# Placing the odd linear product and the mirroring pass within a unit of a fused FNet-mixing and maxout-FFN kernel

## The chip, the cores and the metric

The kernel runs on one core of a Trainium2 chip. The metric is the device time of one execution in microseconds, as the median of several executions. TensorE (PE) multiplies, VectorE (DVE) and ScalarE (ACT) work on what it leaves in PSUM, GpSimd (POOL) works on SBUF and issues some DMAs, and SyncE (SP) issues the other DMAs. Each engine takes its instructions in the order in which the program lists them, and waits on semaphores where one needs another's result.

## The reference

```python
def _attn_ref(x):                        # x: (8, 3072, 256)
    X = np.fft.fft(x, axis=1)
    X = np.fft.fft(X, axis=2)
    return X.real.astype(np.float32)

def _moe_ref(x, w1, w2, w3, w_out):      # x: (24576, 256), w1..w3: (256, 768), w_out: (768, 256)
    h = np.maximum(np.maximum(x @ w1, x @ w2), x @ w3)
    return (h @ w_out).astype(np.float32)
```

The result of the first is the input of the second: 8 batch entries of 3072 tokens, each of 256 values.

## The kernel before

**What is multiplied.** The kernel never forms the mixed tokens in full. The Fourier transform over the 3072 positions leaves, for each batch entry, two tables of 128 rows and 1536 columns, an even part `tE` and an odd part `tO`; the transform over the 256 features is folded into the weights. A token's values come from the even part plus the odd one, and those of its mirror image (position 3072 less its own) from the even part less the odd one. So one column gives two output rows, a "plus" and a "minus" one. The maximum over three products is written as x·w1 + max(0, x·(w2−w1), x·(w3−w1)). The x·w1 part goes straight to the output through one folded matrix (`gw`), and is called the linear part here. The maximum goes through the 768 hidden columns (`hp` for plus, `hm` for minus) and then through `wout_bf`.

**Batch, block, unit, slot.** A batch entry has 1536 columns in 3 blocks of 512. A block is worked in 6 units, one for each 128 of the 768 hidden columns (`jc` 0 to 5), so an entry has 18 units; "unit 0" to "unit 17" below are those of one entry, and `jc` is the unit's number within its block. A block's 512 columns are also 4 slots of 128 columns, and each slot yields 128 plus rows and 128 minus rows of the output.

**A unit's first half** makes the hidden values. `unit_plus` (L491, L492) runs four matmuls of 512 columns: an even and an odd one into the PSUM tile `pse2`, then an even and an odd one into `pse3`. `unit_out` (L505, L506) then lets ACT write relu(`pse2`) to `stmp`, and DVE write max(`pse3`, `stmp`) to `hp`. One unit later, `finish(prev)` runs the two difference products of the previous unit (`unit_minus`, L499), which add −2 times the odd part to the same two PSUM tiles, and a second `unit_out` that writes `hm`. The tiles `pse2` and `pse3` have two buffers each, so a unit's `pse3` cannot be started until DVE has written the `hm` of the unit two before it, which happens within the unit just before.

**A unit's second half** makes output of the block before it. The generator `l2_block` lists, slot by slot, 12 matmuls of 256 columns (`l2_hidden`, L516): 6 from `hp` and 6 from `hm`, added in a PSUM tile `po`. `l2_some(n)` takes the next n steps of that list. Between two slots of a pair `l2_even` (L528, L531) makes the even linear part of two later slots: two matmuls of 256 columns and a copy by ACT into an SBUF tile, noted in `lines`. The odd linear part is `l2_odd`: one matmul of 257 columns (L539), which is the first to write the slot's `po`; then DVE's mirroring pass `other` (L542), which reads that `po`; then POOL's addition (L545), which makes the minus half of the slot's linear part from `other`. The slot's 12 hidden matmuls add into the same `po`, so they wait until `other` has been made. At the slot's end DVE adds `po` and the linear part into `ot` (L567), POOL issues an indirect DMA for the minus rows (L569) and SP issues the plain stores. There are two `po` buffers. The odd product of a slot therefore waits until the `ot` of the slot two before it is done.

**Where `l2_odd` stands before the change.** In a unit the order is: plus products, odd product and mirroring pass, `hp`, difference products, `hm`, hidden matmuls. It is called in the units with `jc` 1, 2, 4 (slots 1, 2, 3 of the block before) and `jc` 5 (slot 0 of the block at work). The very first block has no such calls for its slot 0: `l2_block` itself calls `l2_even` and `l2_odd` there, in the midst of the hidden matmuls.

**What else is in a unit.** The dictionary `plan` hangs pieces of the next entries' transform to a unit's end: the `s` and `k` matmuls (L445, L447, L471, L473) with an eviction by ACT, fetches of input by SP, and `turn_chunk`, the conversions by POOL (L148, L151) that bring the rows of the entry after next into order. For entries 2 to 6 the `s` and `k` pieces lie in units 5 to 17, one each; for entry 1 they begin in unit 6; in entry 0 they begin in unit 10 and run into entry 1. Conversions lie in units 6 to 17 of an entry and in units 0 to 3 of the next, one part each; those of entry 2 lie in unit 14 of entry 0 to unit 3 of entry 1, two parts each. Entry 7 has no pieces but a short side job in units 0 to 5.

The count that `l2_some` takes in a block's units is 9, 9, 8, 9, 9, 8, and what is left is taken after the last unit's pieces.

Of the kernel before, what the change touches and what calls it, by code (L numbers as in the profile page):

```python
# [33 lines left out]
def kernel(  # L34
# [11 lines left out]
    B, S, D = x.shape  # L46
# [438 lines left out]
    def unit_plus(te, to, jc, n):  # L485

        js = slice(jc * 128, (jc + 1) * 128)
        pse2 = ps_l1.tile([128, TOKB], FP32, name="pse2", tag="pse2")
        pse3 = ps_l1.tile([128, TOKB], FP32, name="pse3", tag="pse3")
        for (pse, i) in ((pse2, 0), (pse3, 1)):  # L490
            nc.tensor.matmul(pse[:, 0:n], gE[i][:, js], te, start=True, stop=False)  # L491
            nc.tensor.matmul(pse[:, 0:n], gO[i][:, js], to, start=False, stop=True)  # L492
        return pse2, pse3

    def unit_minus(pses, to, jc):

        js = slice(jc * 128, (jc + 1) * 128)
        for i, pse in enumerate(pses):
            nc.tensor.matmul(pse, gD[i][:, js], to, start=False, stop=True,  # L499
                             skip_group_check=True)  # L500

    def unit_out(pses, dst, n):
        stmp = h_pool.tile([128, TOKB], BF16, name="stmp", tag="stmp")
        src3 = pses[1][:, 0:n]
        nc.scalar.activation(out=stmp[:, 0:n], in_=pses[0][:, 0:n], func=AX.Relu)  # L505
        nc.vector.tensor_tensor(out=dst, in0=src3, in1=stmp[:, 0:n], op=ALU.max)  # L506

    def stored(st, mine, others):
        for group in others:
            tc.declare_no_dep(st.ins, group=group, reason="each store has rows of its own")  # L510
        tc.add_to_no_dep_group(mine, st.ins)

    def l2_hidden(po, hcols):
        for jc in range(NJC):
            yield
            nc.tensor.matmul(po, hcols(jc), wout_bf[:, jc * 256:(jc + 1) * 256],  # L516
                             start=False, stop=(jc == NJC - 1), skip_group_check=True)

    lines = {}
    odd = {}  # L520

    def l2_even(b, slot):

        pl = ps_f.tile([128, 512], FP32, name="pl", tag="ps")
        for i in range(2):
            ci = (slot + i) * 128
            yield
            nc.tensor.matmul(pl[:, i * 256:(i + 1) * 256], mixes[b].tE[:, ci:ci + 128],  # L528
                             gw[:, 0:256], start=True, stop=True)
        even = even_pool.tile([128, 1024], FP32, name="even", tag="even")  # L530
        nc.scalar.copy(out=even.rearrange("p (i c) -> p i c", i=2)[:, :, 0:256],  # L531
                       in_=pl.rearrange("p (i c) -> p i c", i=2))
        for i in range(2):
            lines[b, slot + i] = even[:, i * 512:(i + 1) * 512]

    def l2_odd(b, slot):

        po = ps_o.tile([128, 512], FP32, name="po", tag="po")
        nc.tensor.matmul(po[:, 0:257], mixes[b].tO[:, slot * 128:slot * 128 + 128], gw[:, 256:513],  # L539
                         start=True, stop=True)  # L540
        other = other_pool.tile([128, 256], FP32, name="other", tag="other")
        nc.vector.scalar_tensor_tensor(out=other, in0=twice, scalar=po[:, 256:257],  # L542
                                       in1=po[:, 0:256], op0=ALU.mult, op1=ALU.subtract)
        line = lines[b, slot]
        nc.gpsimd.tensor_tensor(out=line[:, 256:512], in0=line[:, 0:256], in1=other, op=ALU.add)  # L545
        odd[b, slot] = po

    def l2_block(b, blk, hp, hm):

        base = b * S  # L550
        for sub in range(4):
            slot = blk * 4 + sub
            r = slot + 1
            sp = slice(sub * 128, sub * 128 + 128)
            if (b, slot) not in odd:
                yield from l2_even(b, slot)
                l2_odd(b, slot)
            if sub % 2:
                after = (b, slot + 1) if slot < 11 else (b + 1, 0)
                if after < (B - 1, 8):  # L560
                    yield from l2_even(*after)
            lin = lines.pop((b, slot))
            po = odd.pop((b, slot))
            ot = out_pool.tile([128, 512], FP32, name="ot", tag="ot")
            yield from l2_hidden(po[:, 0:256], lambda jc: hp[:, jc, sp])
            yield from l2_hidden(po[:, 256:512], lambda jc: hm[:, jc, sp])
            nc.vector.tensor_tensor(out=ot, in0=po, in1=lin, op=ALU.add)  # L567
            lo = 1 if r == 12 else 0
            stored(nc.gpsimd.indirect_dma_start(  # L569
                out, bass.IndirectOffsetOnAxis(  # L570
                    ap=rows_m[0:128 - lo, b * 12 + slot: b * 12 + slot + 1], axis=0),
                ot[lo:128, 256:512], None), "scattered", ("scattered", "direct"))
            nc.gpsimd.memset(mark, 0.0)
            if r <= 11:
                stores = [(0, 128, base + r)]
            else:
                stores = [(0, 64, base), (64, 128, base + 12)]
            for (p0, p1, row) in stores:
                stored(nc.sync.dma_start(out=out[row: row + 24 * (p1 - p0 - 1) + 1: 24, :],
                                         in_=ot[p0:p1, 0:256]), "direct", ("scattered",))  # L580
# [71 lines left out]
    def l2_some(n):  # L652
        while n > 0 and l2_queue:
            try:
                next(l2_queue[0])
                n -= 1
            except StopIteration:
                l2_queue.pop(0)
# [85 lines left out]
    for b in range(B):  # L744
        mm = mixes[b]
        tE, tO = mm.tE, mm.tO
        prev = None

        def finish(prev):
            pses, to, jc, hm = prev  # L750
            unit_minus(pses, to, jc)
            unit_out(pses, hm[:, jc, ::-1] if hm is last_hm else hm[:, jc, :], TOKB)

        last_hm = None
        if b == B - 1:
            flipped = []
            for t, name in ((tE, "tEr"), (tO, "tOr")):
                fl = h_pool.tile([128, TOKB], BF16, name=name, tag=name)
                flipped.append(fl)
        for blk in range(3):  # L760
            cs = slice(blk * TOKB, (blk + 1) * TOKB)
            hp = h_pool.tile([128, NJC, TOKB], BF16, name="hp", tag="hp")
            hm = h_pool.tile([128, NJC, TOKB], BF16, name="hm", tag="hm")
            if b == B - 1 and blk == 2:
                last_hm = hm
                for t, fl in zip((tE, tO), flipped):
                    nc.gpsimd.tensor_copy(fl, t[:, 3 * TOKB - 1: 2 * TOKB - 1: -1])
            for jc in range(NJC):
                pses = unit_plus(tE[:, cs], tO[:, cs], jc, TOKB)
                nb, nblk = (b, blk) if jc == 5 else (b, blk - 1) if blk else (b - 1, 2)  # L770
                slot = nblk * 4 + {1: 1, 2: 2, 4: 3, 5: 0}.get(jc, 12)
                if slot < 12 and (0, 0) < (nb, slot) < (B - 1, 8):
                    l2_odd(nb, slot)
                unit_out(pses, hp[:, jc, :], TOKB)
                if prev is not None:
                    finish(prev)
                prev = (pses, tO[:, cs], jc, hm)
                l2_some(8 if jc % 3 == 2 else 9)
                if b == B - 1 and blk == 0:
                    if jc == 0:  # L780
                        middle = l2_mid()
                    for _ in range(5):
                        next(middle, None)
                for fn in plan.get((b, blk * NJC + jc), ()):
                    fn()
            l2_some(1000)
            if blk == 2:
                finish(prev)
            l2_queue.append(l2_last(hp, hm, tE, tO, flipped) if b == B - 1 and blk == 2 else
                            l2_block(b, blk, hp, hm))  # L790

    l2_some(1000)
# [29 lines left out]
```

## Time and profile before

| | |
|---|---|
| Median of 3 executions | 426.38 us (426.24 to 426.39) |
| The profiled execution, its own time | 426.3 us |
| Its span, from the first to the last instruction | 424.4 us |
| Granted TensorE clock, mean | 0.999 |
| Time from the start of one entry's units to the same place of the next, entries 2 to 6 | 48.0 us |

The profile is of one execution. Its rows give the start of an instruction in us from the start of the span, its length, and the idle time before it with what ended that idle time. Matmuls overlap: a matmul of 512 columns is shown as 0.38 us long, yet the next one starts 0.21 us after it. So a wait on TensorE is read from the distance between two starts. A few matmul records are missing from the trace; there the distance is simply doubled, and the weight loads show what was lost.

### The profile page before, as it was taken

To read this page: it belongs to the slowest core of one execution; us is meant where nothing else is said; L and a number is where in the kernel's file an instruction comes from. 1 tells how busy PE (TensorE), PEld (TensorE's weight loads), DVE (VectorE), ACT (ScalarE), POOL (GpSimd) and SP (SyncE) were. 2 spreads that over 40 slices of the span, in tenths; PEclk is the share of its full clock that TensorE was granted. 3 is DMA by queue.
4 is the path that set the end of the run, shared out by engine and by line. 5 is a ranking of instruction groups with operands and counts; after the bars stand their busy time and mean duration, and the time that the engine had idled before them with its cause. 6 is when DMAs were issued, how large, how long until landed. Compare 5 with 4: busy or idle time off the path is not lost.

```text
span 424.4 us, 8989 instructions
## 1 busy us (share of the span) xinstructions
PE 401.0 (94%) x3029; PEld 270.2 (64%) x3084; DVE 311.4 (73%) x558; ACT 264.5 (62%) x478; POOL 316.8 (75%) x431
## 2 busy tenths in 40 slices
PE   0899899998999999999999999999999999999996
PEld 0365567665766666666666666666676676765665
DVE  8878577757777776786777776786777777777883
ACT  6856667665765676656675576666675676655550
POOL 9926876999978878878878788888878744446540
PEclk9999999999999999999999999999999999999999
DMA  9998896585216942397315952288312122212214
GB/s 106 100 171 171 167 213 157 141 198 134 88 63 175 204 118 74 92 212 171 110 51 154 219 108 101 79 204 186 109 56 76 62 65 76 76 51 58 93 63 137
DMA packets 131174, 51.90 MB, mean 122 GB/s; under 512 B 113073, under 2 KB 128184, under 8 KB 131128
## 3 DMA queue, kind: packets, MB, share of 16 engines
q1 hardware_dynamic: 105408, 35.93, 35.9%
q0 software_dynamic: 24784, 15.08, 16.5%
q8 instruction: 24, 0.39, 0.4%
q10 hardware_dynamic: 936, 0.33, 0.3%
q14 instruction: 22, 0.18, 0.1%
HBM read 29.02 MB, written 25.17 MB: 128 GB/s over the span
## 4 chain that ended last, share of the span: by engine, by line
PE 88%; DVE 4%; issue 2%; ACT 2%; POOL 1%; DMA 1%; SPq 0%; DVEq 0%; POOLq 0%; ACTq 0%
PE po L516 27%; PE pse L491 16%; PE pse L499 13%; PE pse L492 12%; PE po L539 3%; PE ps L445 3%; PE ps L447 3%; PE ps L473 2%; PE ps L471 2%; PE warm L662 2%; PE pl L528 2%; DVE hm L506 2%; PE psg L385 1%; DMA xs<-in_x_dram 1%; DVE other L542 1%
## 5 line engine op out<-in xcount | busy, mean ns | idle before, releaser
L505 ACT ACTIVATE stmp<-pse 128x512 bf16<-128x512 f32 x288 | 172.0, 599 | 59.1 <-PE pse L492 30.7
L569 POOL DMA_INDIRECT out_dram<-ot,rows_m x92 | 103.1, 1121 | 78.1 <-DVE ot L567 68.5
L506 DVE TENSOR_TENSOR hp<-pse,stmp 128x512 bf16<-128x512 f32 x144 | 98.8, 686 | 29.4 <-ACT stmp L505 17.3
L491 PE MATMUL pse<-t,gE 128*128 128x512 bf16 x288 | 109.2, 379 | 4.8 <-DVE hm L506 1.9
L506 DVE TENSOR_TENSOR hm<-pse,stmp 128x512 bf16<-128x512 f32 x144 | 98.5, 684 | 2.5 <-ACT stmp L505 1.6
L492 PE MATMUL pse<-t,gO 128*128 128x512 bf16 x249 | 94.3, 379 | 0.0
L516 PE MATMUL po<-wout_bf,hm 128*128 128x256 bf16 x570 | 92.0, 273 | 0.0
L542 DVE SCALAR_TENSOR_TENSOR other<-twice,po 128x256 f32<-128x256 f32 x92 | 44.6, 485 | 61.5 <-PE po L539 61.5
L516 PE MATMUL po<-wout_bf,hp 128*128 128x256 bf16 x576 | 86.1, 273 | 1.4 <-DVE other L542 1.3
L499 PE MATMUL pse<-t,gD 128*128 128x512 bf16 x272 | 82.2, 379 | 0.8
L516 PEld LDWEIGHTS <-hp 128*128 128x128 bf16 x576 | 56.3, 98 | 24.8 <-issue 1.5
L545 POOL TENSOR_TENSOR even<-even,other 128x256 f32<-128x256 f32 x92 | 66.5, 724 | 7.2 <-DVE other L542 7.1
L148 POOL CAST x<-xs 96x544 bf16<-96x544 f32 (+2 forms) x52 | 60.6, 1169 | 12.0 <-DMA xs<-in_x_dram 12.0
L516 PEld LDWEIGHTS <-hm 128*128 128x128 bf16 x576 | 56.4, 98 | 19.0 <-issue 0.2
L567 DVE TENSOR_TENSOR ot<-po,even 128x512 f32<-128x512 f32 x92 | 62.8, 683 | 6.6 <-POOL even L545 2.6
L151 POOL CAST x<-xs 96x544 bf16<-96x544 f32 (+5 forms) x59 | 62.3, 1066 | 0.0
L475 ACT CAST t<-ps 128x512 bf16<-128x512 f32 x47 | 27.5, 585 | 31.6 <-PE ps L473 30.7
L499 PEld LDWEIGHTS <-gD 128*128 128x128 bf16 x288 | 28.0, 97 | 25.9 <-issue 5.8
L492 PEld LDWEIGHTS <-gO 128*128 128x128 bf16 x288 | 28.1, 97 | 25.6 <-issue 10.1
L452 ACT CAST z_all<-ps 128x480 bf16<-128x480 f32 x45 | 25.1, 558 | 29.3 <-PE ps L447 28.5
L491 PEld LDWEIGHTS <-gE 128*128 128x128 bf16 x288 | 28.1, 98 | 20.0 <-issue 1.4
L531 ACT COPY even<-pl 128x512 f32<-128x512 f32 x46 | 26.9, 586 | 14.0 <-PE pl L528 7.9
(157 smaller groups left out, 379.9 us busy)
## 6 DMA issues: line engine op xcount, KB each, us to landing
xs<-in_x_dram SPq DMA_DIRECT2D x84, 198.0 KB
out_dram<-ot SPq DMA_DIRECT2D x90, 128.0 KB
xs<-in_x_dram SPq DMA_DIRECT2D x28, 192.0 KB
out_dram<-ot,rows_m POOLq DMA_INDIRECT x92, 3.1
x<-in_x_dram POOLq DMA_DIRECT2D x12, 96.0 KB, 4.2
w_bf<-in_moe_w_dram POOLq DMA_DIRECT2D x6, 192.0 KB, 5.6
out_dram<-ot SPq DMA_DIRECT2D x17, 64.0 KB
xs<-in_x_dram SPq DMA_DIRECT2D x32, 5.8 KB
```

The costliest lines, as they stand in the source:

```text
L148: nc.gpsimd.tensor_copy(v[:, d0:d1, ch * 32:ch * 32 + 32], xs[:, 0:32 * 64].rearrange("p (bb dl) -> p dl bb", dl=64)[:, d0:d1, :])
L151: reverse(lambda out, in_: nc.gpsimd.tensor_copy(out, in_), v[:, 33:66, :], xs, ch * 32, 33 if ch == 3 else 32, 32 + d0, 32 + d1)
L491: nc.tensor.matmul(pse[:, 0:n], gE[i][:, js], te, start=True, stop=False)
L492: nc.tensor.matmul(pse[:, 0:n], gO[i][:, js], to, start=False, stop=True)
L499: nc.tensor.matmul(pse, gD[i][:, js], to, start=False, stop=True, skip_group_check=True)
L505: nc.scalar.activation(out=stmp[:, 0:n], in_=pses[0][:, 0:n], func=AX.Relu)
L506: nc.vector.tensor_tensor(out=dst, in0=src3, in1=stmp[:, 0:n], op=ALU.max)
L516: nc.tensor.matmul(po, hcols(jc), wout_bf[:, jc * 256:(jc + 1) * 256], start=False, stop=(jc == NJC - 1), skip_group_check=True)
L542: nc.vector.scalar_tensor_tensor(out=other, in0=twice, scalar=po[:, 256:257], in1=po[:, 0:256], op0=ALU.mult, op1=ALU.subtract)
L545: nc.gpsimd.tensor_tensor(out=line[:, 256:512], in0=line[:, 0:256], in1=other, op=ALU.add)
L567: nc.vector.tensor_tensor(out=ot, in0=po, in1=lin, op=ALU.add)
L569: stored(nc.gpsimd.indirect_dma_start(out, bass.IndirectOffsetOnAxis(ap=rows_m[0:128 - lo, b * 12 + slot: b * 12 + slot + 1], axis=0), ot[ ...
```

## The change

The call of `l2_odd` is moved from between the plus products and `hp` to behind `finish(prev)`. In a unit the order becomes: plus products, `hp`, difference products, `hm`, odd product and mirroring pass, hidden matmuls. Slots 1 and 3 of a block are served one unit earlier, in `jc` 0 and 3; slot 2 stays in `jc` 2 and the next block's slot 0 in `jc` 5. A call is made only if the slot's even part has been listed, and if fewer than two `po` buffers are still in use by the list (`banks`). The steps of a block's units become 10, 9, 8, 9, 9, 8, one more in the first. Where no call has been made, `l2_block` makes it itself, as before, now also when only the odd part is missing.

```diff
+    banks = set()
...
     def l2_odd(b, slot):
...
         odd[b, slot] = po
+        banks.add((b, slot))
...
             if (b, slot) not in odd:
-                yield from l2_even(b, slot)
+                if (b, slot) not in lines:
+                    yield from l2_even(b, slot)
                 l2_odd(b, slot)
...
             nc.vector.tensor_tensor(out=ot, in0=po, in1=lin, op=ALU.add)
+            banks.remove((b, slot))
...
             for jc in range(NJC):
                 pses = unit_plus(tE[:, cs], tO[:, cs], jc, TOKB)
-                nb, nblk = (b, blk) if jc == 5 else (b, blk - 1) if blk else (b - 1, 2)
-                slot = nblk * 4 + {1: 1, 2: 2, 4: 3, 5: 0}.get(jc, 12)
-                if slot < 12 and (0, 0) < (nb, slot) < (B - 1, 8):
-                    l2_odd(nb, slot)
                 unit_out(pses, hp[:, jc, :], TOKB)
                 if prev is not None:
                     finish(prev)
                 prev = (pses, tO[:, cs], jc, hm)
-                l2_some(8 if jc % 3 == 2 else 9)
+                nb, nblk = (b, blk) if jc == 5 else (b, blk - 1) if blk else (b - 1, 2)
+                slot = nblk * 4 + {0: 1, 2: 2, 3: 3, 5: 0}.get(jc, 12)
+                if (nb, slot) in lines and len(banks) < 2:
+                    l2_odd(nb, slot)
+                l2_some((10, 9, 8, 9, 9, 8)[jc])
```

## The prediction

> **What bounds the kernel.** I read first the page's busy times and groups, then a table of stretches, then TensorE's timeline in the one stretch of an entry where it waits.
>
> ```profile
> PE 401.0 (94%) x3029; PEld 270.2 (64%) x3084; DVE 311.4 (73%) x558; ACT 264.5 (62%) x478; POOL 316.8 (75%) x431
> L569 POOL DMA_INDIRECT out_dram<-ot,rows_m x92 | 103.1, 1121 | 78.1 <-DVE ot L567 68.5
> L542 DVE SCALAR_TENSOR_TENSOR other<-twice,po 128x256 f32<-128x256 f32 x92 | 44.6, 485 | 61.5 <-PE po L539 61.5
> L545 POOL TENSOR_TENSOR even<-even,other 128x256 f32<-128x256 f32 x92 | 66.5, 724 | 7.2 <-DVE other L542 7.1
> L567 DVE TENSOR_TENSOR ot<-po,even 128x512 f32<-128x512 f32 x92 | 62.8, 683 | 6.6 <-POOL even L545 2.6
> ...
> 190.00:240.00 50.00, 49.49 (x386) 34.04 (x392) 37.39 (x64) 32.23 (x60) 41.71 (x56) 1.00 0.52 135
> ...
> 181.00:189.10 8.10, 7.91 (x49) 4.74 (x49) 6.54 (x12) 4.64 (x9) 6.13 (x10) 1.00 0.95 214
> 325.00:333.10 8.10, 7.91 (x49) 4.74 (x49) 6.54 (x12) 4.65 (x9) 6.14 (x10) 1.00 0.18 67
> 403.95:412.05 8.10, 7.91 (x49) 4.73 (x49) 6.54 (x12) 4.06 (x8) 3.56 (x6) 1.00 0.17 65
> ```
>
> TensorE is covered for 49.49 of 50 us, at the full clock. VectorE's mirroring pass idles 61.5 us waiting for the odd product, at the head of an in-order queue, with `hp` behind it. So only TensorE's waits can be won. They are small and hide under overlapping records, so they are read between starts:
>
> ```profile
> 228.78 0.90 PE L491 MATMUL pse<-t,gE 128*128 128x512 bf16 x2
> 229.52 0.38 PE L492 MATMUL pse<-t,gO 128*128 128x512 bf16 x1
> 229.91 0.27 PE L539 MATMUL po<-gw,t 128*128 128x257 bf16 x1
> ...
> 231.53 0.38 PE L492 MATMUL pse<-t,gO 128*128 128x512 bf16 x1
> 231.95 0.38 PE L491 MATMUL pse<-t,gE 128*128 128x512 bf16 x1
> ...
> 234.44 0.38 PE L492 MATMUL pse<-t,gO 128*128 128x512 bf16 x1
> 234.77 0.27 PE L539 MATMUL po<-gw,t 128*128 128x257 bf16 x1
> ...
> 237.03 0.38 PE L492 MATMUL pse<-t,gO 128*128 128x512 bf16 x1
> 237.41 0.27 PE L539 MATMUL po<-gw,t 128*128 128x257 bf16 x1
> ```
>
> Here are units 2 to 5 of one entry, which hold no transform pieces. Undisturbed, a 512-column matmul follows the last by 0.215 us. In unit 2 three of them take 0.74 (229.52−228.78; one record is missing), so `pse3` waited 0.10, and the odd product then waited 0.39−0.215=0.17. Unit 3's `pse3` waits 0.20, unit 4's odd product 0.11, and unit 5 repeats unit 2 (0.10, and 0.17 by its rows). Sum: **0.85 us an entry**. The three short stretches, first and last of entries 3 to 6 and one of entry 7, show the same 49 matmuls with the same cover, so I count it for entries 2 to 6.
>
> ```profile
> 227.57 0.48 DVE L542 SCALAR_TENSOR_TENSOR other<-twice,po 128x256 f32<-128x256 f32 x1 [0.88 <-PE po L539]
> 227.97 0.68 DVE L506 TENSOR_TENSOR hp<-pse,stmp 128x512 bf16<-128x512 f32 x1
> 228.58 0.68 DVE L506 TENSOR_TENSOR hm<-pse,stmp 128x512 bf16<-128x512 f32 x1
> 229.17 0.68 DVE L567 TENSOR_TENSOR ot<-po,even 128x512 f32<-128x512 f32 x1
> ...
> 232.38 0.59 PE L499 MATMUL pse<-t,gD 128*128 128x512 bf16 x2
> ...
> 233.43 0.69 DVE L506 TENSOR_TENSOR hm<-pse,stmp 128x512 bf16<-128x512 f32 x1
> ...
> 234.23 0.38 PE L491 MATMUL pse<-t,gE 128*128 128x512 bf16 x1
> ```
>
> The first four rows are the cause: `other`, `hp`, `hm`, `ot` run in a chain. `hm` ends at 229.26, just ahead of unit 2's late `pse3`; `ot` ends at 229.85, 0.06 before the late odd product.
>
> **The change, part by part.** No instruction is added or removed but for order; no DMA is added, and the indirect DMAs and conversions keep their order on their queues against `ot`.
>
> *Steady units.* I count from a unit's first plus product, T. Four plus products take 0.86, two difference products 0.43, an odd product 0.11, each hidden matmul 0.109 (8 to 9 of them). With the odd product behind them, the difference products start at T+0.86 in each unit, as now only in units without one, like unit 3. There `hm` ended 1.74 after the first difference product started (234.12−232.38), so at T+2.60, and unit 4's `pse3` was not held up: 234.23 is 0.44 after its unit's start. After the change every unit is like that: with 8 hidden matmuls it lasts 0.86+0.43+0.11+0.87=2.27, the next `pse3` is due at T+2.70, and the buffer is free at T+2.66, with the same 0.06. Cover: 0.04. The three waits for `pse3` go.
>
> The waits for a `po` buffer: the odd product is now 0.43 later in its unit. Slot 2's and slot 0's buffers come from an `ot` of the unit before, which follows `hm` there (T+2.51 to 3.19) and is due at 2.27+1.29=3.56: no wait. Slot 3's buffer, in unit 3, comes from the `ot` at the end of unit 2. That stands behind `hm` and, newly, `other`: VectorE starts one 512-column pass 0.60 after another (228.58 to 229.17), one 0.40 after `other`, so `other` is at T+2.51 and `ot` at T+2.91 to 3.59. With 0.06 the odd product starts at 3.65 where it was due at 3.56: **0.1 us is left**. Gain 0.75 an entry, times 5: **−3.75**. If the cover of 0.04 fails by 0.05 in four units, 0.2 an entry comes back (−2.75); nothing but the 0.85 can be won (−4.25).
>
> The Trainium skill, "VectorE: DVE Perf Modes", "The DRAIN you can't avoid", speaks against this: a VectorE operation does not start before the one ahead of it has left the pipe. The rows here start 0.08 early (`hm` at 228.58 while `hp` runs to 228.65). By the rule each of the chained passes would start some 0.08 later, the wait in unit 3 would be about 0.3, and the gain 0.2 an entry smaller.
>
> *Entry 7* has no pieces, so the pattern comes twice (0.85 and, without the last, 0.68), and once more singly at the block's border, 0.1: 1.6. After: 0.1 each in units 9, 12 and 15. **−1.3** (0 to −1.6).
>
> *The first block*, in units 6 to 11 of entry 0. In unit 6 slot 1 has no even part listed yet, so the moved call is passed over, and the list itself makes slot 1's odd product in unit 7. In unit 9 both buffers are in use, so slot 3's falls into the list in unit 10. There its 12 hidden matmuls follow at once, behind two even ones (0.22), and must wait for `other`, which now stands behind `hp`, `hm` and the previous slot's `ot`.
>
> ```profile
> 44.98 0.81 PE L516 MATMUL po<-wout_bf,hp 128*128 128x256 bf16 x6 [1.32 <-DVE other L542]
> 46.07 0.38 PE L491 MATMUL pse<-t,gE 128*128 128x512 bf16 x1
> ...
> 48.03 1.42 POOL L545 TENSOR_TENSOR even<-even,other 128x256 f32<-128x256 f32 x2
> ...
> 48.84 0.68 DVE L567 TENSOR_TENSOR ot<-po,even 128x512 f32<-128x512 f32 x1
> ...
> 48.86 0.23 PE L473 MATMUL ps<-tab,z_all 128*128 128x128 bf16 x1
> 49.18 0.17 PE L481 MATMUL ps<-tab,z_all 128*128 128x2 bf16 x1
> ```
>
> Slot 0, made in the list already, shows the kind of wait: 1.32. Unit 7 starts at 46.07+0.11 (unit 6 takes one more hidden matmul); 1.29 of products, 5 hidden, one odd and two even ones end at 48.35. `ot` cannot start before 48.84, as POOL's addition for slot 0 stays where it is; `other` follows at 49.45 and ends at 49.93: 1.6 us. In unit 10 `hm` starts at T+1.91, `ot` at 2.51, `other` at 3.11 to 3.59, and TensorE is there at 0.86+0.43+0.55+0.11+0.22=2.17: 1.5 us. Against these 3.1 stand 0.26 that unit 7's `k` piece no longer waits (0.32 from 48.86 to 49.18, where 128 columns take half of 0.109), and 0.3 for the waits of units 9 and 10, if they follow the steady pattern (0.20 and 0.11). **+2.6** (from 1.3, if one of the two falls under other work, to 3.6).
>
> *Entry 1*, where conversions come two a unit:
>
> ```profile
> 65.40 0.81 PE L491 MATMUL pse<-t,gE 128*128 128x512 bf16 x2
> ...
> 90.33 0.38 PE L491 MATMUL pse<-t,gE 128*128 128x512 bf16 x1
> ...
> 93.00 2.30 POOL L151 CAST x<-xs 96x561 bf16<-96x561 f32 x3
> 95.28 0.72 POOL L545 TENSOR_TENSOR even<-even,other 128x256 f32<-128x256 f32 x1
> ...
> 96.03 0.69 DVE L567 TENSOR_TENSOR ot<-po,even 128x512 f32<-128x512 f32 x1 [2.59 <-POOL even L545]
> ...
> 97.97 0.38 PE L491 MATMUL pse<-t,gE 128*128 128x512 bf16 x1 [1.93 <-DVE hm L506]
> ...
> 95.23 0.21 PE L445 MATMUL ps<-m24f,x 96*128 96x96 bf16 x1
> ```
>
> Slot 3's addition stood behind the last conversions, its `ot` waited 2.59, `hm` behind it, and TensorE 1.9; with some 0.35 in units 5 and 6, by the steady pattern, that is 2.25. The addition now comes a unit earlier, ahead of those conversions (2.30), but POOL starts the row of conversions later: unit 14's stand behind an `ot` that ends at T+3.59 and its DMA. From there POOL has that DMA (1.1), seven pairs of conversions of about 2.1 (the 2.30 above holds a small third one), five additions of 0.7 and four more DMAs of 1.12 with gaps of 0.16: 3.6+0.3+1.1+14.8+3.5+5.1=28.4 after unit 14's start. VectorE wants that `ot` at 24.9+2.91=27.8 (unit 5 started 24.93 after unit 14). So 0.6 of wait; and the first `s` piece, which started at 95.23 just as its conversion ended, waits some 0.3. **−1.35** (0 to −2.25).
>
> Sum: −3.75−1.3+2.6−1.35=−3.8. The profiled execution took 426.3 (span 424.4 and 1.9 around it), 0.1 under the median: **422.5 us**, span about 420.6. Its own range, with any one term at its bound, is 421.2 to 423.9.
>
> **The rivals.**
> (a) The list's two waits cost little and entry 1's wait goes wholly: −4.25−1.6+1.3−2.25=−6.8, 419.5. Against it: slot 0's 1.32.
> (b) Half is won: cover fails (−2.75), entry 1 keeps its wait (0): −1.45, 424.9.
> (c) The waits only change places, the odd product waiting 0.43 later for the same `ot`: the first block's 2.6 stands against entry 1's and some of the rest, 426 to 427. Against it: three of the six waits are not for `po`.
> (d) Slower: POOL becomes the bound. An addition comes about 0.9 later in its unit, since `other` does, and conversions and DMAs queue behind it.
>
> ```profile
> 236.04 1.21 POOL L151 CAST x<-xs 96x495 bf16<-96x495 f32 x2
> ...
> 238.82 0.21 PE L445 MATMUL ps<-m24f,x 96*128 96x96 bf16 x1
> ```
>
> The last conversion ends at 237.25, 1.57 ahead of the `s` piece that reads it; beyond 1.57 each us is TensorE's. If three additions hold the queue 0.9 each, 2.7−1.57=1.1 for five entries and 2.7 in entry 1: −3.8+5.5+2.7=+4.4, 430.7. Against it: POOL has 41.7 of 50 us busy, and a slot's addition is not wanted before the slot's end.
> (e) The guard refuses more than the first block's call: a list-made product costs about 1.5, for 22 blocks 33 us, 455. Against it: with ten steps in the first unit slot 1's `ot` is listed as the last step of unit 2, so one buffer is in use at unit 3.
> (f) The drain rule holds: 0.2 for five entries and 0.6 in entry 7, 424.1.
>
> **How the numbers follow.** Forecast 60%, (a) 8, (b) 14, (c) 4, (d) 8, (e) 3, (f) 3. Some 0.2% (0.85 us) can be told from no change. Faster: forecast, (a), (f) and 10 of (b), 81; same: 4 of (b) and 3 of (c), 7; slower 12. The range 419.3 to 425.6 takes in (a), (b) and (f).
>
> **What would show it.** In units 2 to 5 of a middle entry the starts of matmuls lie 0.215 apart but for 0.1 ahead of unit 3's odd product: right. Two waits near 1.5 of hidden matmuls for `other` in units 7 and 10 of entry 0, beside slot 0's. `ot` in entry 1's unit 5 waits for POOL by 0.6 instead of 2.59. I am wrong if `pse3` still waits each unit, if `s` pieces wait for POOL in entries 2 to 6, or if list-made products come in later blocks.

## The result and the profile after

| | before | after |
|---|---|---|
| Median, runs shown | 426.34 us (426.24 to 426.39) | 422.14 us (422.0 to 422.84) |
| Ratio after to before, 95% interval | | 0.9905 (0.9888 to 0.9922) |
| Span of the profiled execution | 424.4 us | 420.3 us |

The page of the changed kernel: busy times of the engines, and three of its groups; the row of the mirroring pass is from the list of groups by line; the last row is the same stretch as before, in the columns stretch, its length, and busy us of PE, weight loads, DVE, ACT and POOL, then clock and DMA.

```profile
PE 396.6 (94%) x3029; PEld 270.3 (64%) x3084; DVE 310.7 (74%) x558; ACT 263.3 (63%) x478; POOL 318.1 (76%) x431
L506 DVE TENSOR_TENSOR hp<-pse,stmp 128x512 bf16<-128x512 f32 x144 | 99.5, 691 | 92.5 <-ACT stmp L505 63.7
L573 POOL DMA_INDIRECT out_dram<-ot,rows_m x92 | 103.2, 1121 | 55.7 <-DVE ot L570 43.9
L570 DVE TENSOR_TENSOR ot<-po,even 128x512 f32<-128x512 f32 x92 | 62.8, 682 | 0.5 <-POOL even L546 0.3
...
L543 DVE SCALAR_TENSOR_TENSOR other<-twice,po 128x256 f32<-128x256 f32 x92 | 43.8, 476 | 0.0
...
190.00:240.00 50.00, 49.63 (x391) 34.42 (x396) 37.83 (x65) 32.72 (x61) 41.56 (x56) 1.00 0.53 136
```

The mirroring pass no longer idles at the head of VectorE's queue (61.5 us before, none now); VectorE's idle time lies ahead of `hp` instead, 92.5 us, of which 63.7 are spent waiting for ScalarE; the list of TensorE's own waits names no `hp`. TensorE does more in the same 50 us: 396 weight loads where there were 392.

Where the 4.1 us of span came from is seen by laying the starts of the same unit's first plus product side by side. These are TensorE's rows (weight loads where a matmul record is missing), in us:

| Entry, unit | before | after | difference |
|---|---|---|---|
| 0, unit 6 | 41.88 | 41.90 | +0.02 |
| 0, unit 8 | 49.28 | 50.65 | +1.37 |
| 0, unit 12 | 59.99 | 62.41 | +2.42 |
| 1, unit 0 | 77.38 | 79.91 | +2.53 |
| 2, unit 0 | 128.09 | 129.12 | +1.03 |
| 3, unit 0 | 176.66 | 176.94 | +0.28 |
| 4, unit 0 | 224.66 | 224.37 | −0.29 |
| 5, unit 0 | 272.66 | 271.62 | −1.04 |
| 6, unit 0 | 320.66 | 318.87 | −1.79 |
| 7, unit 0 | 368.66 | 366.12 | −2.54 |
| end of span | 424.4 | 420.3 | −4.1 |

The first block loses 2.4 and the rest of entry 0 another 0.1; entry 1 wins 1.5, entries 2 to 6 win 0.75 each (entry 3 0.57), entry 7 wins 1.6.

TensorE's timeline in units 2 and 3 of entry 4, two of the four units whose waits the prediction counted (start, length, engine, line, operation, tiles):

```profile
229.25 0.38 PE L492 MATMUL pse<-t,gO 128*128 128x512 bf16 x1
229.46 0.59 PE L499 MATMUL pse<-t,gD 128*128 128x512 bf16 x2
229.90 0.27 PE L540 MATMUL po<-gw,t 128*128 128x257 bf16 x1
...
231.09 0.38 PE L492 MATMUL pse<-t,gO 128*128 128x512 bf16 x1
231.31 0.38 PE L491 MATMUL pse<-t,gE 128*128 128x512 bf16 x1
...
231.74 0.59 PE L499 MATMUL pse<-t,gD 128*128 128x512 bf16 x2
232.25 0.27 PE L540 MATMUL po<-gw,t 128*128 128x257 bf16 x1
```

Unit 2's odd product starts 0.44 after the first difference product (229.90−229.46), where two products take 0.43: no wait. Unit 3's `pse3` starts 0.22 after the matmul ahead of it (231.31−231.09): no wait either, where 0.20 stood before. The one wait left is ahead of unit 3's odd product: 232.25−231.74 is 0.51, 0.08 more than two products take. Units 4 and 5 show none by their starts. VectorE's rows of the same time give its cause:

```profile
230.51 0.69 DVE L506 TENSOR_TENSOR hm<-pse,stmp 128x512 bf16<-128x512 f32 x1
231.12 0.48 DVE L543 SCALAR_TENSOR_TENSOR other<-twice,po 128x256 f32<-128x256 f32 x1
231.51 0.69 DVE L570 TENSOR_TENSOR ot<-po,even 128x512 f32<-128x512 f32 x1
```

`other` starts 0.61 after `hm`, `ot` 0.39 after `other` and ends at 232.20, 0.05 ahead of the odd product that takes its buffer. Unit 2 started at 228.60, so `hm` ended at 2.60 and `ot` at 3.60 after it.

The two products of the first block that the list makes, in units 7 and 10 of entry 0, by TensorE's and VectorE's rows:

```profile
48.16 0.38 PE L529 MATMUL pl<-gw,t 128*128 128x256 bf16 x2
49.85 0.38 PE L516 MATMUL po<-wout_bf,hp 128*128 128x256 bf16 x2 [1.32 <-DVE other L543]
...
57.15 0.38 PE L529 MATMUL pl<-gw,t 128*128 128x256 bf16 x2
58.84 0.38 PE L516 MATMUL po<-wout_bf,hp 128*128 128x256 bf16 x2 [1.31 <-DVE other L543]
...
48.73 0.68 DVE L570 TENSOR_TENSOR ot<-po,even 128x512 f32<-128x512 f32 x1
49.33 0.48 DVE L543 SCALAR_TENSOR_TENSOR other<-twice,po 128x256 f32<-128x256 f32 x1
...
PE po L516 <- DVE other L543: 3.9, 3, 1.3
```

Two even products take 0.22; the hidden ones start 1.69 after the first of them, so TensorE lost 1.47 each time, until `other` ended behind `ot`. The last row is from the list of TensorE's waits (total us, times, longest): there are three waits of this kind in the whole execution, slot 0's, which the kernel before has too, and these two.

Entry 1, units 5 and 6, by GpSimd's, VectorE's and TensorE's rows:

```profile
95.51 0.72 POOL L546 TENSOR_TENSOR even<-even,other 128x256 f32<-128x256 f32 x1
96.18 2.33 POOL L151 CAST x<-xs 96x561 bf16<-96x561 f32 x3
...
96.26 0.69 DVE L570 TENSOR_TENSOR ot<-po,even 128x512 f32<-128x512 f32 x1 [0.29 <-POOL even L546]
...
97.00 0.27 PE L540 MATMUL po<-gw,t 128*128 128x257 bf16 x1 [0.29 <-DVE ot L570]
...
98.09 0.21 PE L445 MATMUL ps<-m24f,x 96*128 96x96 bf16 x1
98.39 0.22 PE L447 MATMUL ps<-m24r,x 96*128 96x96 bf16 x1
```

Slot 3's addition now runs ahead of the last conversions. Its `ot` waits 0.29 for it (2.59 before), the odd product starts 0.89 after the first difference product where 0.43 is due, so 0.46 is lost there. In the first `s` piece two matmuls of 96 columns start 0.29 apart (98.09 to 98.39 as rounded in the rows) where the following ones start 0.04 apart, so 0.25 is lost there, until the second of the three conversions has ended (98.33).

### The profile page after: what moved, and what is told of

Its sections match the earlier page's. It is cut to its first block, busy times and chain, and to the rows that moved or that the text cites. A ratio compares the mean times of both kernels' runs of the same rounds, so it can differ in the third digit from the quotient of the medians.

```text
span 420.3 us, 9060 instructions
## 1 busy us (share of the span) xinstructions
PE 396.6 (94%) x3029; PEld 270.3 (64%) x3084; DVE 310.7 (74%) x558; ACT 263.3 (63%) x478; POOL 318.1 (76%) x431
## 4 chain that ended last, share of the span: by engine, by line
PE 91%; DVE 2%; ACT 2%; issue 2%; POOL 2%; DMA 1%; DVEq 0%; ACTq 0%; POOLq 0%
PE po L516 29%; PE pse L491 16%; PE pse L499 14%; PE pse L492 12%; PE ps L445 3%; PE ps L447 3%; PE po L540 3%; PE ps L473 2%; PE ps L471 2%; PE pl L529 2%; PE warm L666 2%; PE psg L385 1%; ACT stmp L505 1%; DMA out_dram<-ot 1%; POOL x L151 1%
## 5 line engine op out<-in xcount | busy, mean ns | idle before, releaser
L506 DVE TENSOR_TENSOR hp<-pse,stmp 128x512 bf16<-128x512 f32 x144 | 99.5, 691 | 92.5 <-ACT stmp L505 63.7
L516 PE MATMUL po<-wout_bf,hm 128*128 128x256 bf16 x570 | 85.6, 273 | 0.2
```

## The experiments

The theory: the gain needs both halves of the change. The mirroring pass must stand behind `hm`, so that it does not delay the buffers that TensorE takes up next; and it must come a unit earlier, since behind `hm` it ends too late for a slot whose hidden matmuls begin in the same unit. The rivals: one half alone does it, or the pass is not on TensorE's path at all. Each edit is shown against the changed kernel (the pass made twice also against the kernel before); `...` marks lines left out.

**The order alone** (old units, old counts):

```diff
-                slot = nblk * 4 + {0: 1, 2: 2, 3: 3, 5: 0}.get(jc, 12)
+                slot = nblk * 4 + {1: 1, 2: 2, 4: 3, 5: 0}.get(jc, 12)
-                l2_some((10, 9, 8, 9, 9, 8)[jc])
+                l2_some(8 if jc % 3 == 2 else 9)
```

> The new order within a unit alone: the odd product behind the difference products, but in the old units (jc 1, 2, 4, 5) and with the old counts of steps. Theory (both halves of the change are needed): in units 1 and 4 of a block the slot's hidden matmuls come in the same unit, 0.86+0.43+0.11+0.44+0.22 = 2.06 us after its start, while the mirroring pass behind both maxima ends at about 2.99, so TensorE waits some 0.95 twice a block, 23 blocks: about +44 us, less the 3 us of the first block's two list-made products: 463 us (455 to 470). Rival (the order alone brings the gain): 422 us, within 1.

Measured: 462.97 us, ratio to before 1.0862 (1.0844 to 1.088). In the list of TensorE's waits of this kernel (total us, times, longest):

```profile
PE po L516 <- DVE other L543: 39.1, 47, 1.3
```

These are two waits in each of 23 blocks and slot 0's. The view counts a wait from the shown end of the last matmul; between starts each costs some 0.16 more, so about 1.0 where 0.95 was expected. The order without the earlier unit costs 36.7 us, nearly nine times what the whole change gains.

**The units alone** (slots a unit earlier and the new counts, but the odd product ahead of `hp`):

```diff
                 pses = unit_plus(tE[:, cs], tO[:, cs], jc, TOKB)
+                nb, nblk = (b, blk) if jc == 5 else (b, blk - 1) if blk else (b - 1, 2)
+                slot = nblk * 4 + {0: 1, 2: 2, 3: 3, 5: 0}.get(jc, 12)
+                if (nb, slot) in lines and len(banks) < 2:
+                    l2_odd(nb, slot)
                 unit_out(pses, hp[:, jc, :], TOKB)
...
-                nb, nblk = (b, blk) if jc == 5 else (b, blk - 1) if blk else (b - 1, 2)
-                slot = nblk * 4 + {0: 1, 2: 2, 3: 3, 5: 0}.get(jc, 12)
-                if (nb, slot) in lines and len(banks) < 2:
-                    l2_odd(nb, slot)
```

> The new units and counts of steps alone: slots 1 and 3 a unit earlier, but the odd product ahead of hp as before the change. Theory: the mirroring pass is again ahead of hp, hm and ot, and waits of some 0.1 to 0.2 us come back in units 2 to 5, about 0.6 us an entry against 0.08 now: +2.8 us for entries 2 to 6 and about +1.1 in entry 7, 426 us (424.5 to 427). Rival (serving the slots a unit earlier is what helps, wherever the pass stands): 422 us, within 0.7.

Measured: 428.27 us, ratio 1.0046 (1.0029 to 1.0063): 1.9 slower than before, and 1.3 above the top of what was expected. TensorE's and VectorE's rows of this kernel in units 2 and 3 of entry 4, and the row of its waits for `other`:

```profile
231.03 0.38 PE L492 MATMUL pse<-t,gO 128*128 128x512 bf16 x1
231.36 0.27 PE L540 MATMUL po<-gw,t 128*128 128x257 bf16 x1
...
232.99 0.38 PE L492 MATMUL pse<-t,gO 128*128 128x512 bf16 x1
233.41 0.38 PE L491 MATMUL pse<-t,gE 128*128 128x512 bf16 x1
233.62 0.38 PE L492 MATMUL pse<-t,gO 128*128 128x512 bf16 x1
234.00 0.27 PE L540 MATMUL po<-gw,t 128*128 128x257 bf16 x1
...
231.67 0.49 DVE L543 SCALAR_TENSOR_TENSOR other<-twice,po 128x256 f32<-128x256 f32 x1 [0.36 <-PE po L540]
232.07 0.68 DVE L506 TENSOR_TENSOR hp<-pse,stmp 128x512 bf16<-128x512 f32 x1
232.67 0.68 DVE L506 TENSOR_TENSOR hm<-pse,stmp 128x512 bf16<-128x512 f32 x1
233.27 0.68 DVE L570 TENSOR_TENSOR ot<-po,even 128x512 f32<-128x512 f32 x1
...
PE po L516 <- DVE other L543: 3.9, 3, 1.3
```

The old chain `other`, `hp`, `hm`, `ot` is back, and with it 0.11 ahead of unit 2's odd product (0.33−0.215), 0.20 ahead of unit 3's `pse3` and 0.17 ahead of its odd product (0.38−0.215). Unit starts show 0.78 more than the changed kernel in entries 4 to 6 (0.96 in entry 2) where 0.56 was expected, 0.17 of it a wait in unit 12 that was not counted, and 2.1 more in entry 7 (1.1 expected). That the rival falls is clear; the mechanism was right and its total undersized.

Against the kernel before, this half alone is neither a gain nor a loss in the steady entries: entries 3 to 6 take 48.03 here and 48.00 there, with waits of 0.86 in entry 4 where the prediction had read 0.85. They have changed their places. The 1.9 us come from elsewhere: this kernel has the two list-made products too (the last row), and loses 2.9 in entry 0 by unit starts; it wins 1.6 in entry 1 and loses 0.5 in entry 7.

**The first block in the old way:**

```diff
+                if (b, blk) == (0, 1) and jc in (1, 2, 4):
+                    l2_odd(0, {1: 1, 2: 2, 4: 3}[jc])
                 unit_out(pses, hp[:, jc, :], TOKB)
...
-                if (nb, slot) in lines and len(banks) < 2:
+                if (b, blk, jc) not in ((0, 1, 2), (0, 1, 3)) and (nb, slot) in lines and len(banks) < 2:
```

> The changed kernel, but in the first block (units 6 to 11 of entry 0) the odd products of slots 1 to 3 stand where they stood before the change. Theory: the two waits of 1.49 and 1.48 us go and some 0.5 of small ones come back, and nothing later takes it up: 419.7 us (419.2 to 420.4). Rival (entry 1, where GpSimd's conversions are late, takes the gain back): 421 to 422.2 us.

Measured: 419.64 us, ratio 0.9846 (0.983 to 0.9863). The same list of waits holds slot 0's alone now:

```profile
PE po L516 <- DVE other L543: 1.3, 1, 1.3
```

Nothing later took the 2.5 back: each unit start from unit 12 of entry 0 on is 2.6 to 2.8 ahead of the changed kernel's (0.1 of it from before unit 6). The two waits were a price that the change paid without need.

**The pass made twice, in the changed kernel and in the kernel before:**

```diff
+        for _ in range(2):
-        nc.vector.scalar_tensor_tensor(out=other, in0=twice, scalar=po[:, 256:257],
-                                       in1=po[:, 0:256], op0=ALU.mult, op1=ALU.subtract)
+            nc.vector.scalar_tensor_tensor(out=other, in0=twice, scalar=po[:, 256:257],
+                                           in1=po[:, 0:256], op0=ALU.mult, op1=ALU.subtract)
```

> The changed kernel with the mirroring pass made twice (0.40 us more of VectorE for each of the 92 slots). Theory: the pass lies beside TensorE's work but for unit 3's wait for its po buffer and the three list-made products of the first block: 8 times 0.40 there and 3 times 0.40 here, and some 0.05 in blocks with transform pieces: +4.4 to +5.5 us, 427 us (425.5 to 428.5). Rival (the pass is wholly off the path): 422.1 to 423.3. Rival (VectorE as a whole is the bound, so all 92 passes count): 422.1 + 92 x 0.40 = 459 us.

Measured, changed kernel: 434.3 us, ratio to the unaltered kernel before 1.019 (1.0173 to 1.0207). That is 12.2 above the changed kernel and none of the three expectations. VectorE's rows of units 2 and 3 of entry 4, and TensorE's of unit 6:

```profile
235.94 0.69 DVE L506 TENSOR_TENSOR hm<-pse,stmp 128x512 bf16<-128x512 f32 x1
236.55 1.00 DVE L544 SCALAR_TENSOR_TENSOR other<-twice,po 128x256 f32<-128x256 f32 x2
237.47 0.68 DVE L571 TENSOR_TENSOR ot<-po,even 128x512 f32<-128x512 f32 x1
...
245.14 0.59 PE L499 MATMUL pse<-t,gD 128*128 128x512 bf16 x2
245.74 0.27 PE L540 MATMUL po<-gw,t 128*128 128x257 bf16 x1
```

The pair takes 0.92 of the queue (237.47−236.55) where one took 0.39, so the second costs 0.52 to 0.53, not 0.40. It starts only when the first has ended (1.00 for both, 0.48 for one), whereas the passes of the chain start 0.08 before that. The second writes the same tile as the first; that this is the reason is likely, but no run here shows it. And in unit 6, which holds a transform piece, the odd product waits 0.17 (0.60−0.43). By the distances of starts this wait comes in every odd product of `jc` 0 and `jc` 3 in blocks with pieces (0.41 in unit 12), and unit 3's is 0.60. The expectation had counted unit 3 alone. What is learned: in the changed kernel these odd products have 0.35 us (0.52−0.17) to spare, unit 12's only 0.11, and no more.

> The kernel before the change with the mirroring pass made twice (0.52 us more of VectorE each, as the changed kernel with it twice showed). Theory: before the change the pass heads the chain other, hp, hm, ot, so its cost is TensorE's in every unit that has one: about 0.5 in the odd-product units without transform pieces (4 an entry in units 0 to 5, all 8 of units 6 to 17 of entry 7) and about 0.15 in the others, where hm has some 0.4 to spare: 10 + 4 + 7 = +20 us, 446 (438 to 452), against +12.2 in the changed kernel. Rival (the place of the pass is no matter, it costs the same in both): 438.5, within 1.

Measured, kernel before: 456.18 us, ratio 1.0699 (1.0682 to 1.0716), 29.8 above. Its waits of TensorE:

```profile
PE pse L491 <- DVE hm L506: 11.0, 30, 0.6
```

The same 0.52 costs 29.8 at the old place and 12.2 at the new one. The rival (the place does not matter) is out. The size was again above what was expected (20): units without pieces wait 0.44 and 0.72 for `pse3`, but 0.17 to 0.42 is lost in each unit with pieces too, among it 0.17 of the hidden matmuls of slots 1 and 3, which wait for `other`.

**Entry 2's conversions one unit earlier:**

```diff
-                    at(b, 6 + 4 * ch + part if b else 14 + 2 * ch + part // 2,
+                    at(b, 6 + 4 * ch + part if b else 13 + 2 * ch + part // 2,
```

> The changed kernel with entry 2's conversions a unit earlier (units 13 to 20 in place of 14 to 21), which takes GpSimd's backlog out of entry 1. Theory: entry 1's two waits of 0.46 (po buffer, behind an ot that waits for GpSimd) and 0.29 (first s piece) go: 421.4 us (421.2 to 421.8). Rival (these waits are another's than the conversions'): 422.1, within 0.3.

Measured: 422.92 us, ratio 0.9916 (0.9902 to 0.993), 0.8 slower than the changed kernel: a miss of the expectation's sign. GpSimd's and VectorE's rows of this kernel:

```profile
94.26 2.33 POOL L151 CAST x<-xs 96x561 bf16<-96x561 f32 x3
96.55 0.71 POOL L546 TENSOR_TENSOR even<-even,other 128x256 f32<-128x256 f32 x1
...
97.30 0.69 DVE L570 TENSOR_TENSOR ot<-po,even 128x512 f32<-128x512 f32 x1 [1.27 <-POOL even L546]
```

The last conversions moved from behind slot 3's addition to ahead of it. They began earlier, at 94.26 in place of 96.18, but only 1.3 of this is idle time of GpSimd put to use (it had waited 1.30 ahead of the addition that starts at 71.08 in the changed kernel); the rest is the place of the addition that they overtook. So the addition came at 96.55 in place of 95.51, and `ot` waited 1.27 in place of 0.29. That made the theory sharper: on a full in-order queue it is what stands ahead of the needed instruction that counts.

**The conversions three units earlier** (`11 + 2 * ch + part // 2` in the same line):

> The changed kernel with entry 2's conversions three units earlier (units 11 to 18), into the time in which GpSimd still idles in entry 0. With them one unit earlier slot 3's addition in unit 3 of entry 1 fell behind the last conversions (2.33 us) and came at 96.55 in place of 95.51. Theory (what counts is how much of the conversions is listed ahead of that addition and how long GpSimd idled before): the last conversions are done by about 89, the addition comes as soon as its mirroring pass, and both waits of entry 1 (0.46 and 0.29) go: 421.4 us (421.1 to 421.7). Rival (the later chunks of input have not landed, GpSimd waits for them and loses as much): 422 to 423.

Measured: 421.48 us, ratio 0.9899 (0.9874 to 0.9923); one of the six executions took 424.66, the others 421.15 to 421.59. GpSimd's rows in entry 1:

```profile
87.65 2.33 POOL L151 CAST x<-xs 96x561 bf16<-96x561 f32 x3
...
93.14 0.73 POOL L546 TENSOR_TENSOR even<-even,other 128x256 f32<-128x256 f32 x1
```

The conversions end at 89.98 and the addition comes 2.4 earlier than in the changed kernel. Unit 7 of entry 1 starts at 98.05 where the changed kernel has 98.78 (0.09 of this lies before the entry's waits): both waits are gone but for the 0.08 of the steady units. The order of the medians agrees (421.48 and 422.14), but the intervals of the two ratios overlap; it is the profile that shows the waits gone.

**Combinations.** The first block in the old way with the conversions one unit earlier; the same, with slot 2 taken out of the dictionary (`{0: 1, 3: 3, 5: 0}`), so that the list makes slot 2's odd product at the end of unit 2; and that with the conversions from unit 11 on.

> Both: the first block's odd products in their old place, and entry 2's conversions a unit earlier. Theory: the gains add, 419.64 - 0.75 = 418.9 us (418.6 to 419.3). Rival (one takes the other's cover): 419.4 to 419.9.

> As best, but slot 2's call is left out, so that the list makes its odd product at the end of unit 2, behind slot 1's ot. Theory: ot then ends at T+3.19 in place of 3.59, and unit 3's wait of 0.08 for its po buffer goes, five times in entries 2 to 6 and three times in entry 7, 0.6 us: 418.3 (418.0 to 418.7). Rival (slot 2's hidden matmuls, due 3.67 after unit 2's start, come before its mirroring pass has ended at about 3.65): a new wait of up to 0.1 takes its place, 418.9, or more in units with 8 hidden matmuls.

> First block in the old way, conversions from unit 11 on, and slot 2's odd product made by the list at the end of unit 2. Theory: 419.64 - 0.75 for entry 1 - 0.5 for unit 3's wait: 418.4 us (418.0 to 418.9). Rival (in the shorter entry 0 the input for the conversions is late): 419 to 420.

Measured: 420.43 us (ratio 0.9862, 0.9847 to 0.9878), 420.08 (0.9849, 0.9834 to 0.9865) and 418.75 (0.9824, 0.9811 to 0.9837). The first two carry the ill-placed conversions; their expectations, made before that was seen, missed by 1.5 and 1.8. Leaving slot 2 to the list took unit 3's 0.08 out of entries 2 to 6, 0.07 an entry by unit starts, but for 0.23 that unit 3 of entry 3 takes longer than in the other entries, a place where the changed kernel loses 0.25 too; the medians of those two runs are 0.35 apart with overlapping intervals. The last came within its range and is the fastest of the study, 7.6 us under the kernel before. Its TensorE in the stretch shown above:

```profile
190.00:240.00 50.00, 50.00 (x398) 34.41 (x396) 37.05 (x64) 32.68 (x60) 41.48 (x54) 1.00 0.52 137
```

## Why the prediction was right, point by point

Its terms against the shifts of unit starts and the waits seen (us):

| Term | forecast | measured |
|---|---|---|
| Steady units, entries 2 to 6 | −3.75 | −3.57 (four entries −0.75, entry 3 −0.57) |
| Entry 7 | −1.3 | −1.6 |
| First block | +2.6 | +2.4 |
| Entry 1 | −1.35 | −1.5 |
| Rest of entry 0 | not counted | +0.1 |
| Sum | −3.8 | −4.1 in span, −4.2 in medians |

The mechanism was right in each term, and each term missed by at most 0.3. That the sum came within 0.4 owes a little to luck, as the misses lie on both sides: the steady units won 0.2 less than forecast, the other three terms came out 0.15 to 0.3 better.

- **Steady units.** The wait left ahead of unit 3's odd product was forecast at 0.1 and is 0.08; `hm` ended 2.60 after its unit's start, and the cover of 0.04 for `pse3` held in every entry but one. In entry 3 the `hp` of unit 2 started 0.25 after its `stmp` had ended, and unit 3 then lost 0.25 in two waits, ahead of `pse3` and of the odd product, where the other entries lose 0.08. What delayed it the runs do not show.
- **That both halves are needed** was argued in the prediction only through the two kinds of wait. The order alone cost 36.7 us; the units alone left the steady entries as they were (48.03 against 48.00) and lost 1.9, for the most part by the first block's two waits; both together gain 4.2, with these two waits in it.
- **First block.** 1.6 and 1.5 were forecast for the two list-made products, 1.47 was lost in each. The prediction's own rows give 1.58 (49.93−48.35) and 1.42 (3.59−2.17), and less the 0.56 that stand against them 2.44; its 2.6 is rounded up. The first was a little too large because POOL's addition for slot 0 was taken to stay in its place; `ot` started at 48.73 instead of 48.84. The experiment that undid this part gave 2.5 back.
- **Entry 1.** 0.6 for the `po` buffer and 0.3 for the `s` piece were forecast, 0.46 and 0.25 came; `ot` waited 0.29 for GpSimd, where 0.6 was named as the sign. That the cause is how GpSimd's queue is ordered was an argument there; the two runs that moved the conversions show it, one by making it worse.
- **Entry 7.** The small waits at unit 7 and 13 and in the side job's units were left out of the sum, 0.2 together by the starts, and went too.
- **The rivals.** (a) fell because the list's two waits cost 1.47 each and entry 1 kept 0.7, (b) because the cover held and entry 1 won 1.5. (c) fell with the `pse3` waits, which are gone without others in their place. (d), GpSimd as the bound, was not seen in entries 2 to 6; in entry 1 it is real, for 0.7 us. (e): the waits for `other` number three. (f), the drain rule: passes here start 0.08 before the one ahead has ended (231.12 against 231.20), and the wait that the rule made 0.3 is 0.08. The section of the Trainium skill that the prediction names ("VectorE: DVE Perf Modes", "The DRAIN you can't avoid") goes on to say that an operation which is not held starts earlier, and the prediction left this out; the passes of this chain agree with that sentence and not with the bare rule.

## What to carry to other kernels

In an in-order queue a small operation that waits for a late input should stand behind those whose results another engine takes up next, and its input should be made early enough that it is still in time for its own reader: here the order alone was much slower, the earlier unit alone left the steady entries as they were, and both together gained. When TensorE shows 99% busy, look at the distance between starts, where waits of 0.1 us that repeat each batch can be read and added up. When calls are moved by a rule, look at the places where the rule does not apply (here one block of 23): they took back 2.4 of the 6.6 us won elsewhere.

## What the runs showed of the hardware that was not expected

A second mirroring pass that writes the same tile as the one ahead of it started only when that one had ended and took 0.52 us of VectorE's queue, where `ot` follows the single pass after 0.39. And shifting work earlier on GpSimd, which in this stretch runs without idle time but for gaps of 0.16, made the kernel 0.8 us slower: it gained only the 1.3 us that GpSimd had idled ahead of it, and put 2.33 us of conversions in front of the addition that TensorE's chain needs.
